# One norm extraction for a pair of second-layer weight blocks, and moved steps of attention tiles

## The chip, the cores and the metric

One Trainium2 chip, one core. The metric is the device time of one execution in microseconds (us). The engines are TensorE (matmul; PE in the profile, PEld for its weight loads), VectorE (DVE), ScalarE (ACT), GpSimd (POOL) and SyncE (SP, whose queue issues nearly all DMAs).

## The reference

```python
# attention: batch 2, 8 heads, 576 positions, head width 64, the 32 largest scores of a row kept
scores = matmul(q, k.T) / 8
kth = partition(scores, -32)[..., -32]
scores = where(scores >= kth, scores, -1e9)
attn = exp(scores - max); attn = attn / (sum(attn) + 1e-9)
x = (attn @ v)            # -> 1152 tokens x 512
# first layer pair, 512 -> 2048 -> 512
h = x @ w_in
x = (maximum(h, 0) + alpha * minimum(h, 0)) @ w_out
# second layer pair, 512 -> 1536 -> 512
out = ((x @ w_a) * (x @ w_b)) @ w_out2
```

## The kernel before

Three strands of work run side by side and are written into one program by a small planner (`step`, at the end): it keeps a clock for each strand, always takes the strand whose clock with its shift (`SHIFT_ATT`, `SHIFT_BG`) is lowest, and thereby gives out the instructions in an order. The compiler's scheduler then orders each engine's queue by that order as a priority, among what is ready by its own estimate of times; `tc.high_priority(offset=HPM)` moves the instructions inside it ahead by HPM places.

Strand `dve_track` holds the conversion of the weights and attention. The weights come as 64-bit words of 128 x 512 blocks. `to_f32` loads one block (`raw`, L190), makes the low part on ScalarE (`rlo`, L195 and L196), shifts the high part on VectorE (L197) and adds on GpSimd (L198). There are 68 blocks: 16 each of `wi` and `wo` (first layer), 12 each of `wa`, `wb` and `w2` (second). `CONV` is their order. `square` multiplies a block by its own transpose on TensorE (`gram`, L210) and takes the sum of the diagonal with one VectorE instruction (`junk`, L215), the extraction. Blocks of `wi` and `wo` share one sum for two blocks; each block of `wa` and `wb` has an extraction of its own out of a shared bank and `prep_out` adds the two; each block of `w2` has its own gram and extraction. `w2` blocks don't stay in SBUF: they are stored to DRAM (`w_st`, L222) from one of three slots (`w2s`, W2B = 3), and loaded again (L743) into the same slots when the second layer reads them. The grams share two PSUM banks (tag Y) with the layers' accumulators.

Attention goes through 72 tiles of 128 query rows. `middle` is the search on VectorE: four times the eight largest (L451, L460) and three times their replacement (L458), with a step boundary k = 0 to 7 after each; then masking (L467), the sum's reciprocal, and the normalised row on GpSimd (L474). While tile i is searched, other tiles' work is given out at fixed steps: the scores of the next tile (`front`, L440, copied by L443) at KFRONT; the transposes of the tile before (`back`, L501 to L504) and, at a pair's end, the product with v (`av`, L535) at KBACK. For the second batch ("lifted" tiles, from tile 36 on) the transpose is a DMA (L496) at KLIFT, and the product (L530) comes in the tile after that, at KAV. `v_pair` loads and splits v of the second batch for two heads, in the tiles that V_AT names, at step KV.

Strand `mlp` holds the layers, in six groups of 128 or 256 tokens: `moe1` (L615, L619 and L627, L630 for the two products) and `moe2` (hab or ha and hb, then o). Their epilogues on ScalarE, VectorE and GpSimd (`r`, `gp_n`, `gt`, `gp`) are the instructions under HPM; the end of a group, `finish` (`yb`, L690 to L706), is under HPY = 0. Strand `bg` splits converted weights in two 16-bit halves (`pair`) after the first groups have used them.

Of the kernel before, what the change touches and what calls it, by code (L numbers as in the profile page):

```python
# [11 lines left out]
BF16 = mybir.dt.bfloat16  # L12
# [5 lines left out]
ALU = mybir.AluOpType  # L18

P = 128  # L20
# [5 lines left out]
NF1 = F1 // P  # L26
NF2 = F2 // P
# [1 line left out]
NEG = -3.0e38  # L29

LIFT = 2.0 ** 14
KLIFT = 3
KAV = 3
KV = 4
V_AT = {20: 0, 26: 1, 38: 2, 40: 3}
NORM = "pool"
RLOB = 3
W2B = 3
# [8 lines left out]
JB = 1  # L47
# [15 lines left out]
M2M = 'ppd'  # L63
F0 = 1
HPY = 0
HPM = 100
SB = 2
KBACK = 2
KFRONT = 2
SHIFT_ATT = 4.0  # L70
SHIFT_BG = 4.0
T_PAIR = 4.0
T_ATT = 6.1
# [1 line left out]
F_PE = 1.1  # L75

STEPS = 9
CONV = [(n, i) for i in range(NF1) for n in ("wi", "wo")] + [(n, i) for i in range(NF2) for n in ("wa", "wb", "w2")]
PASSES = ((0, 0), (0, 1), (1, 0))
NBLK = {"wi": NF1, "wo": NF1, "wa": NF2, "wb": NF2, "w2": NF2}  # L80

NPART = {"wi": NF1 // 2, "wo": NF1 // 2, "wa": NF2 // 2, "wb": NF2 // 2, "w2": NF2}


@with_exitstack
def tile_topk_attention_moe(ctx: ExitStack, tc: tile.TileContext, qT, kT, vM, vL, wi, wo, al, wa, wb, w2, out):
    nc = tc.nc
    cp = ctx.enter_context(tc.tile_pool(name="cp", bufs=1))
    sp = ctx.enter_context(tc.tile_pool(name="sp", bufs=2))
# [4 lines left out]
    def psum(name, tag="H"):  # L94
        return pp.tile([P, 512], F32, tag=tag, name=name, bufs=2)

    def small(name, k=1):
        return cp.tile([P, k], F32, tag=name, name=name)

    ident = cp.tile([P, P], F32, tag="ident", name="ident")  # L100
# [11 lines left out]
    def pow2(ssq, scale, inv, k):  # L112
        e2 = sp.tile([P, k], I32, tag=f"e2_{k}", name="e2", bufs=2)
        nc.vector.tensor_scalar(e2[:, 0:k], ssq.bitcast(I32), 1, 0x7F800000, op0=ALU.logical_shift_right, op1=ALU.bitwise_and)
        nc.vector.tensor_scalar(scale.bitcast(I32), e2[:, 0:k], -1, 204 << 23, op0=ALU.mult, op1=ALU.add)
        nc.vector.tensor_scalar(inv.bitcast(I32), e2[:, 0:k], 50 << 23, None, op0=ALU.add)

    def totals(part, k):
        ps = psum("tot")
        nc.tensor.matmul(ps[:, 0:k], ones, part, start=True, stop=True)  # L120
        t = sp.tile([P, NF1], F32, tag="tot", name="tot_s", bufs=2)
        nc.vector.tensor_copy(t[:, 0:k], ps[:, 0:k])
        return t[:, 0:k]
# [4 lines left out]
    def row_max(dst, part):  # L128
        m = sp.tile([P, 2], F32, tag="rm", name="rm", bufs=2)
        fold(m[:, 0:1], part, ALU.max)  # L130
        ps = psum("rmt")
        nc.tensor.matmul(ps[0:1, 0:P], m[:, 0:1], ident, start=True, stop=True)
        fold(m[0:1, 1:2], ps[0:1, 0:P], ALU.max)
        ps2 = psum("rmb")
        nc.tensor.matmul(ps2[:, 0:1], ones[0:1, :], m[0:1, 1:2], start=True, stop=True)
        nc.vector.tensor_copy(dst, ps2[:, 0:1])
# [29 lines left out]
    wsb, wsc, winv, parts = {}, {}, {}, {}  # L166
    for name in ("wi", "wo", "wa", "wb"):
        wsb[name] = cp.tile([P, NBLK[name], DM], F32, tag=f"{name}_sb", name=f"{name}_sb")
    all_parts = small("parts", sum(NPART.values()))
    k0 = 0  # L170
    for name, nb in NBLK.items():
        parts[name] = all_parts[:, k0:k0 + NPART[name]]
        k0 += NPART[name]
        k = 1 if name in ("wo", "w2") else nb // 2
# [4 lines left out]

    def w2_tile():  # L180
        return sp.tile([P, DM], F32, tag="w2s", name="w2s", bufs=W2B)
    cols = {"s": small("cols", 2 * NF2)}
    srcs = {"wi": wi, "wo": wo, "wa": wa, "wb": wb, "w2": w2}
    w2_tiles = {}

# [2 lines left out]
    def to_f32(dst, name, i):  # L188
        raw = early.tile([P, DM], I64, tag="raw", name="raw", bufs=RAWB)
        nc.sync.dma_start(raw, srcs[name][i])  # L190
        lo = raw.bitcast(U32).rearrange("p (n t) -> p n t", t=2)[:, :, 0]
        hi = raw.bitcast(I32).rearrange("p (n t) -> p n t", t=2)[:, :, 1]
        d = dst.bitcast(I32)
        r = early.tile([P, DM], I32, tag="rlo", name="rlo", bufs=RLOB)
        nc.scalar.activation(r.bitcast(I16).rearrange("p (n t) -> p n t", t=2)[:, :, 0], lo, AF.Copy, scale=2.0 ** -29)  # L195
        nc.scalar.activation(r.bitcast(BF16).rearrange("p (n t) -> p n t", t=2)[:, :, 1], hi.bitcast(F32), AF.Sign)  # L196
        nc.vector.tensor_scalar(d, hi, 3, None, op0=ALU.logical_shift_left)  # L197
        nc.gpsimd.tensor_tensor(out=d, in0=d, in1=r, op=ALU.add)  # L198

    def square(name, i, src, n):
        own = name in ("wa", "wb")
        gram = psum("gram", "Y")
        w = src.bitcast(BF16).rearrange("p b (n t) -> p b n t", t=2)[:, :, :, 1]
        for f in range(n):
            d = gram[:, f * P:(f + 1) * P] if own else gram[:, 0:P]
            for c in range(4):
                x = w[:, f, c * P:(c + 1) * P]
                nc.tensor.matmul(d, x, x, start=c == 0 and (own or f == 0), stop=c == 3 and (own or f == n - 1))  # L210
        k = 2 * i + (NF2 if name == "wb" else 0)
        for f in range(2 if own else 1):
            to = cols["s"][:, k + f:k + f + 1] if own else parts[name][:, i:i + 1]
            junk = sp.tile([P, P], BF16, tag="junk", name="junk", bufs=JB)
            nc.vector.scalar_tensor_tensor(junk, gram[:, f * P:(f + 1) * P], 4.125, ident, op0=ALU.mult, op1=ALU.mult, accum_out=to)  # L215

    def block(name, i):
        if name == "w2":
            t = w2_tile()
            to_f32(t, name, i)  # L220
            square(name, i, t.unsqueeze(1), 1)
            nc.sync.dma_start(w2_st[i], t)  # L222
        else:
            to_f32(wsb[name][:, i], name, i)
            if i % 2:
                square(name, i // 2, wsb[name][:, i - 1:i + 1], 2)

    def halves(name, f):
        v = (w2_tiles[f] if name == "w2" else wsb[name][:, f]).bitcast(F16)
# [2 lines left out]
    def scales(name, common):  # L232
        nb = NPART[name]
        t = totals(parts[name], nb)
        if common:
            q = sp.tile([P, 2], F32, tag="rm", name="fold", bufs=2)
            fold(q[:, 0:1], t, ALU.add)
            pow2(q[:, 0:1], wsc[name], winv[name], 1)
        else:
            pow2(t, wsc[name], winv[name], nb)  # L240
        nc.vector.tensor_scalar(wsc[name], wsc[name], 2.0, None, op0=ALU.mult)
        return t
# [59 lines left out]
        nc.vector.tensor_mul(back_y, back_y, winv["wo"][:, 0:1])  # L302

    def prep_out():
        for j, name in enumerate(("wa", "wb")):
            s = cols["s"][:, j * NF2:(j + 1) * NF2].rearrange("p (n t) -> p n t", t=2)
            nc.vector.tensor_add(parts[name], s[:, :, 0], s[:, :, 1])
        scales("wa", False)
        scales("wb", False)
        scales("w2", True)  # L310

        q = small("pq", 4)
        ab = small("pab", NF2)
        nc.vector.tensor_mul(ab, cols["s"][:, 0:NF2], cols["s"][:, NF2:2 * NF2])
        row_max(q[:, 0:1], ab)
        pow2(q[:, 0:1], q[:, 1:2], q[:, 2:3], 1)
        nc.vector.tensor_scalar(q[:, 1:2], q[:, 1:2], 2.0 ** -30, None, op0=ALU.mult)
        nc.vector.tensor_scalar(pre["wa"], winv["wa"], q[:, 1:2], None, op0=ALU.mult)
        nc.vector.tensor_scalar(back_o, winv["w2"][:, 0:1], q[:, 2:3], 2.0 ** 30, op0=ALU.mult, op1=ALU.mult)
# [53 lines left out]
    for g, grp in enumerate(M1):  # L373
# [6 lines left out]
        for part, hp in [(p, h) for p in ((grp[:1], grp[1:]) if lead else (grp,)) for h in range(4)]:  # L380
# [6 lines left out]
            for unit in units:  # L387
                pts_of = {}
                for slot, (kind, b, t) in enumerate(unit):
                    n = P if kind == "T" else D  # L390
# [157 lines left out]
    def attention():  # L548
# [11 lines left out]
        for i, tl in enumerate(tiles):  # L560
            s = ready.pop(0)
            for k, _ in enumerate(middle(tl, s)):
                if k == 0 and i + FA < len(tiles):
                    fetch(tiles[i + FA])
                if k == 1 and i + VA < len(tiles):
                    fetch_v(tiles[i + VA])
                if k == KV and i in V_AT:
                    v_pair(V_AT[i])
                if k == KAV and due:
                    p = due.pop(0)  # L570
                    av(p)
                    yield ("done", p[0]["g"], len(p))
                if prev is not None and k == (KLIFT if prev["lift"] else KBACK):
                    back(prev)
# [4 lines left out]
                    elif prev["last"]:  # L579
                        av(pr)  # L580
                        yield ("done", prev["g"], len(pr))
                        pr = []
                if k == KFRONT and i + QA < len(tiles):
                    ready.append(front(tiles[i + QA]))
# [49 lines left out]
    def moe1(g, s1, s2):  # L634
# [9 lines left out]
        def l1(fc):  # L644
# [6 lines left out]
            contract(h, "wi", fc, xT, n, s1)  # L651
            with tc.high_priority(offset=HPM):
                if s2:
# [76 lines left out]
    def moe2(gs, s3, s4):  # L730
# [32 lines left out]
        def l3(f):  # L763
# [10 lines left out]
            for g, yT, t0 in parts:  # L774
                n = gsize[g]
                va, vb = ha[:, t0 * P:t0 * P + n], hb[:, t0 * P:t0 * P + n]
                with tc.high_priority(offset=HPM):
                    a = sized("r1", 2, n, s4)
# [60 lines left out]
    clock = {"dve": 0.0, "mlp": 0.0, "bg": 0.0}  # L839
# [16 lines left out]
    def dve_track():  # L856
        att = attention()
        cnt = [0] * len(M1)
        need = [sum(1 for t in tiles if t["g"] == g) for g in range(len(M1))]
        order = iter(CONV)  # L860

        def convert():
            name, i = next(order)
            block(name, i)
            conv_done[name, i] = clock["dve"] + T_CONV
            if (name, i) == CONV[-1]:
                open_late()
# [83 lines left out]
    live = {"dve", "mlp", "bg"}  # L951
    shift = {"dve": -SHIFT_ATT, "mlp": 0.0, "bg": SHIFT_BG}

# [8 lines left out]
            clock[k] += r  # L962
        return True

    clock["bg"] = 50.0
    while live:
        step(min(live, key=lambda k: clock[k] + shift[k]))

# [41 lines left out]
```

## Time and profile before

| what | us |
|---|---|
| median of 3 runs | 708.64 |
| lowest and highest | 707.94, 713.67 |
| the profiled execution | 712.79 |
| its span, first to last instruction | 711.0 |
| busy in the span: TensorE, VectorE | 613.9, 565.2 |
| busy in the span: ScalarE, GpSimd | 471.2, 441.9 |

The span is one execution. Times inside it are compared with each other; its own 712.79 us belongs to it and lies above the median of the runs. A busy time is a mean over stretches with different limits.

### The profile page before, as it was taken

The numbers are of one execution on the slowest core, as the hardware profiler recorded it, in microseconds if no ns is written. First come the engines' busy times: TensorE is split into PE (matmuls) and PEld (weight loads), VectorE is DVE, ScalarE is ACT, GpSimd is POOL, SyncE is SP. The second block draws the span as 40 slices with busy tenths as digits, with TensorE's granted clock in tenths as the row PEclk, the third lists the DMA queues.
The fourth block names the chain that finished last, engine by engine and source line by source line (L and its number), as shares of the span: only waits on it lengthen the run. The fifth ranks groups of instructions, "written<-read, shape, count | busy, mean of one in ns | idle before, by whom it ended". The sixth has DMA issues, their size and how long they took to land.

```text
span 711.0 us, 14959 instructions
## 1 busy us (share of the span) xinstructions
PE 613.9 (86%) x5094; PEld 458.4 (64%) x5094; DVE 565.2 (79%) x1450; ACT 471.2 (66%) x979; POOL 441.9 (62%) x648
## 2 busy tenths in 40 slices
PE   2455758899989897979976999999799999999997
PEld 1344545678766576756745777775777766677775
DVE  3998899879889989888999889999999998321021
ACT  4867988797588977789788644466555555543232
POOL 5766788888466667779888854565366555223221
PEclk9976669999989998999998999999899999999999
DMA  6986899895440031222267754523245622001243
GB/s 169 326 236 197 305 318 292 285 359 161 141 123 25 12 84 53 81 73 79 77 196 198 186 143 98 122 42 65 42 102 111 135 54 51 18 2 45 74 130 109
DMA packets 98493, 94.58 MB, mean 133 GB/s; under 512 B 50416, under 2 KB 72688, under 8 KB 98416
## 3 DMA queue, kind: packets, MB, share of 16 engines
q1 hardware_dynamic: 97104, 91.26, 45.3%
q10 hardware_dynamic: 1312, 2.36, 1.1%
q8 instruction: 40, 0.66, 0.4%
q14 instruction: 37, 0.30, 0.1%
HBM read 74.33 MB, written 8.65 MB: 117 GB/s over the span
## 4 chain that ended last, share of the span: by engine, by line
PE 54%; DVE 19%; ACT 10%; DMA 8%; issue 5%; POOL 2%; SPq 1%; ACTq 0%; POOLq 0%; DVEq 0%
PE hab L615 14%; PE h L615 7%; PE o L627 7%; PE y L627 6%; DVE wk L458 5%; DVE m L460 4%; PE ps L440 3%; PE o L535 3%; PE o L630 2%; PE hb L619 2%; DMA kr<-in_kT_dram 2%; PE ha L619 2%; DVE e L467 2%; PE o L530 2%; PE y L630 2%
## 5 line engine op out<-in xcount | busy, mean ns | idle before, releaser
L460 DVE MAX8 m<-wk 128x8 f32<-128x576 f32 x216 | 163.0, 755 | 2.2
L606 POOL TENSOR_TENSOR gp<-gt,gp 128x256 f16<-128x256 f32 (+1 forms) x112 | 67.5, 610 | 84.9 <-ACT gp L605 73.5
L458 DVE MATCH_REPLACE8 wk<-m,wk 128x576 f32<-128x576 f32 x144 | 106.9, 742 | 0.0
L615 PE MATMUL h<-xT,wi_sb 128*128 128x256 f16 (+1 forms) x960 | 97.1, 254 | 3.5 <-ACT xT L543 1.6
L615 PEld LDWEIGHTS <-wi_sb 128*128 128x128 f16 x960 | 79.3, 99 | 22.9 <-issue 9.5
L627 PEld LDWEIGHTS <-gp 128*128 128x128 f16 x588 | 54.8, 98 | 56.4 <-POOL gp L606 3.3
L627 PE MATMUL y<-wo_sb,gp 128*128 128x512 f16 x336 | 81.5, 380 | 2.8 <-POOL gp L606 1.6
L474 POOL TENSOR_SCALAR e<-e,sm 128x576 f32<-128x576 f32 x72 | 54.7, 760 | 45.0 <-DVE sm L472 40.6
L440 PE MATMUL ps<-ks,qh 128*128 128x288 f32 x160 | 48.0, 383 | 30.8 <-DVE e L467 21.7
L615 PE MATMUL hab<-xT,wa_sb 128*128 128x256 f16 (+1 forms) x648 | 69.0, 254 | 1.3 <-ACT xT L706 1.1
L451 DVE MAX8 m<-s 128x8 f32<-128x576 f32 x72 | 54.1, 752 | 18.0 <-ACT s L443 17.4
L605 ACT ACTIVATE gp<-gt 128x256 f16<-128x256 f32 (+1 forms) x112 | 42.2, 388 | 38.5 <-DVE gt L788 18.4
L615 PE MATMUL hab<-xT,wb_sb 128*128 128x256 f16 (+1 forms) x648 | 67.0, 251 | 0.0
L615 PEld LDWEIGHTS <-wa_sb 128*128 128x128 f16 x648 | 54.4, 100 | 14.7 <-issue 1.5
L627 PE MATMUL o<-w2s,gp 128*128 128x512 f16 x252 | 62.8, 379 | 1.0 <-DMA w2s<-w_pr 0.9
L788 DVE SCALAR_TENSOR_TENSOR gt<-hab,wb_inv,r 128x256 f32<-128x256 f32 (+1 forms) x36 | 15.6, 434 | 60.3 <-ACT r L782 60.2
L467 DVE SCALAR_TENSOR_TENSOR e<-s,m,ep 128x576 f32<-128x576 f32 x72 | 58.1, 808 | 3.9 <-PE t L503 1.3
L615 PEld LDWEIGHTS <-wb_sb 128*128 128x128 f16 x648 | 53.1, 99 | 5.8 <-issue 0.4
L195 ACT ACTIVATE rlo<-raw 128x512 int16<-128x512 uint32 x68 | 53.8, 792 | 4.1 <-DMA raw<-in_wi_dram 3.0
L464 ACT ACTIVATE ep<-s,nb 128x576 f32<-128x576 f32 x72 | 53.9, 749 | 3.4 <-DVE e L467 1.7
L782 ACT ACTIVATE r<-hab,pre_wa 128x256 f32<-128x256 f32 (+1 forms) x48 | 21.4, 445 | 51.0 <-PE hab L615 51.0
L440 PEld LDWEIGHTS ps<-ks,qh 128*128 128x128 f32 x160 | 28.6, 210 | 40.7 <-DVE e L467 20.3
(206 smaller groups left out, 1462.3 us busy)
## 6 DMA issues: line engine op xcount, KB each, us to landing
w2s<-w_pr SPq DMA_DIRECT2D x48, 256.0 KB, 2.7
w2s<-w_st SPq DMA_DIRECT2D x36, 256.0 KB, 2.8
raw<-in_wi_dram SPq DMA_DIRECT2D x16, 512.0 KB, 7.0
raw<-in_wo_dram SPq DMA_DIRECT2D x16, 512.0 KB, 6.8
raw<-in_wa_dram SPq DMA_DIRECT2D x12, 512.0 KB, 5.0
raw<-in_wb_dram SPq DMA_DIRECT2D x12, 512.0 KB, 5.1
raw<-in_w_dram SPq DMA_DIRECT2D x12, 512.0 KB, 5.0
kr<-in_kT_dram SPq DMA_DIRECT2D x32, 144.0 KB, 3.1
```

The lines of the kernel that those rows point to most:

```text
L195: nc.scalar.activation(r.bitcast(I16).rearrange("p (n t) -> p n t", t=2)[:, :, 0], lo, AF.Copy, scale=2.0 ** -29)
L440: nc.tensor.matmul(ps[:, f, 0:HALF], q[:, h % 2, :], ks[h][:, f * HALF:(f + 1) * HALF], start=i == 0, stop=i == len(mm) - 1)
L451: nc.vector.max(m8[:, 0:8], s)
L458: nc.vector.match_replace(out=wk, in_to_replace=m8[:, 8 * r - 8:8 * r], in_values=src, imm_value=NEG)
L460: nc.vector.max(m8[:, 8 * r:8 * r + 8], wk)
L464: nc.scalar.activation(ep, w2(s), AF.Exp, bias=nb, scale=0.125)
L467: nc.vector.scalar_tensor_tensor(w2(e), w2(s), m8[:, 31:32], ep, op0=ALU.is_ge, op1=ALU.mult, accum_out=sm[:, 0:1])
L474: nc.gpsimd.tensor_scalar(e, e, sm[:, 1:2], 1.0, op0=ALU.mult, op1=ALU.mult)
L605: nc.scalar.activation(h[:, 0:n], t[:, 0:n], AF.Copy)
L606: nc.gpsimd.tensor_sub(l[:, 0:n], t[:, 0:n], h[:, 0:n])
L615: nc.tensor.matmul(dst[:, 0:n], w[a][:, c * P:(c + 1) * P], x[:, b, c, 0:n], start=k == 0, stop=k == 11)
L627: nc.tensor.matmul(dst, act[b][:, s], w[a], start=i == 0 and k == 0, stop=i == last and k == 2)
```

## The change

Each pair of blocks of `wa`, `wb` and `w2` now shares one sum: one gram of eight matmuls into one place and one extraction, as for `wi` and `wo`; 34 extractions instead of 52. The second-layer conversions come in pairs of blocks (wa, wa, wb, wb, w2, w2), and of `w2` the first block's slot is kept until the second is there. Eight constants of the planner change.

```diff
-KLIFT = 3
-KAV = 3
-KV = 4
-V_AT = {20: 0, 26: 1, 38: 2, 40: 3}
+KLIFT = 4
+KAV = 2
+KV = 6
+V_AT = {22: 0, 28: 1, 38: 2, 40: 3}
-HPM = 100
+HPM = 400
-KBACK = 2
-KFRONT = 2
-SHIFT_ATT = 4.0
+KBACK = 4
+KFRONT = 1
+SHIFT_ATT = 3.0
-CONV = [...] + [(n, i) for i in range(NF2) for n in ("wa", "wb", "w2")]
+CONV = [...] + [(n, i) for j in range(0, NF2, 2) for n in ("wa", "wb", "w2") for i in (j, j + 1)]
-NPART = {..., "wa": NF2 // 2, "wb": NF2 // 2, "w2": NF2}
+NPART = {..., "wa": NF2 // 2, "wb": NF2 // 2, "w2": NF2 // 2}
-    def square(name, i, src, n):
-        own = name in ("wa", "wb")
+    def square(name, i, src):
         gram = psum("gram", "Y")
...
-        for f in range(2 if own else 1):
-            to = cols["s"][:, k + f:k + f + 1] if own else parts[name][:, i:i + 1]
-            junk = sp.tile([P, P], BF16, tag="junk", name="junk", bufs=JB)
-            nc.vector.scalar_tensor_tensor(junk, gram[:, f * P:(f + 1) * P], 4.125, ident, op0=ALU.mult, op1=ALU.mult, accum_out=to)
+        for f, t in enumerate(src):
+            w = t.bitcast(BF16).rearrange("p (n t) -> p n t", t=2)[:, :, 1]
+            for c in range(4):
+                x = w[:, c * P:(c + 1) * P]
+                nc.tensor.matmul(gram[:, 0:P], x, x, start=c == 0 and f == 0, stop=c == 3 and f == len(src) - 1)
+        junk = sp.tile([P, P], BF16, tag="junk", name="junk", bufs=JB)
+        nc.vector.scalar_tensor_tensor(junk, gram[:, 0:P], 4.125, ident, op0=ALU.mult, op1=ALU.mult, accum_out=parts[name][:, i:i + 1])
+    held = []
     def block(name, i):
         if name == "w2":
             t = w2_tile()
             to_f32(t, name, i)
-            square(name, i, t.unsqueeze(1), 1)
             nc.sync.dma_start(w2_st[i], t)
+            held.append(t)
         else:
             to_f32(wsb[name][:, i], name, i)
-            if i % 2:
-                square(name, i // 2, wsb[name][:, i - 1:i + 1], 2)
+            held.append(wsb[name][:, i])
+        if i % 2:
+            square(name, i // 2, held[-2:] if name == "w2" else [wsb[name][:, i - 1], wsb[name][:, i]])
     def prep_out():
-        for j, name in enumerate(("wa", "wb")):
-            s = cols["s"][:, j * NF2:(j + 1) * NF2].rearrange("p (n t) -> p n t", t=2)
-            nc.vector.tensor_add(parts[name], s[:, :, 0], s[:, :, 1])
...
-        ab = small("pab", NF2)
-        nc.vector.tensor_mul(ab, cols["s"][:, 0:NF2], cols["s"][:, NF2:2 * NF2])
+        ab = small("pab", NF2 // 2)
+        nc.vector.tensor_mul(ab, parts["wa"], parts["wb"])
-    clock["bg"] = 50.0
+    clock["bg"] = 30.0
```

## Rows read from the trace of the kernel before

**Rows 1.** Busy time by stretch: from:to, length, PE, PEld, DVE, ACT, POOL, clock, DMA.

```profile
98.00:126.60 28.60, 18.57 (x116) 13.68 (x114) 28.60 (x67) 23.24 (x49) 25.64 (x29) 0.86 0.91 294
126.60:200.00 73.40, 71.25 (x554) 56.91 (x555) 61.83 (x201) 58.69 (x127) 55.23 (x68) 0.98 0.69 228
200.00:400.00 200.00, 174.30 (x1412) 129.62 (x1410) 180.55 (x453) 167.07 (x340) 151.59 (x236) 0.94 0.34 93
400.00:602.00 202.00, 195.93 (x1650) 143.31 (x1648) 194.44 (x466) 108.54 (x225) 113.31 (x184) 0.98 0.43 93
```

**Rows 2.** Chain of waits in order of time: start, us, what.

```profile
126.62 2.07 PE h L619 x8
...
609.80 0.90 PE o L530 x27
```

**Rows 3.** Groups of VectorE instructions: count, busy us, mean ns of one, idle before.

```profile
L460 DVE MAX8 m<-wk 128x8 f32<-128x576 f32 x216 | 163.0, 755 | 2.2
...
L215 DVE SCALAR_TENSOR_TENSOR junk<-gram,ident 128x128 bf16<-128x128 f32 x52 | 14.6, 280 | 6.4 <-PE gram L210 6.2
```

**Rows 4.** VectorE in order of time: start us, us, what.

```profile
115.68 0.28 DVE L215 SCALAR_TENSOR_TENSOR junk<-gram,ident 128x128 bf16<-128x128 f32 x1
...
115.96 1.52 DVE L197 TENSOR_SCALAR w2s<-raw 128x512 int32<-128x512 int32 x1
```

**Rows 5.** GpSimd in order of time at the same place.

```profile
115.91 1.29 POOL L198 TENSOR_TENSOR wb_sb<-wb_sb,rlo 128x512 int32<-128x512 int32 x1 [0.93 <-ACT rlo L196]
```

**Rows 6.** Waits of TensorE from 99 us on: us in total, times, longest.

```profile
PE tp L705 <- ACT yb L700: 5.9, 4, 4.3
PE ps L440 <- DVE e L467: 5.1, 3, 3.2
PE h L619 <- DVE gp_n L669: 3.6, 2, 2.4
...
PE o L530 <- DMA pt<-e: 2.9, 3, 2.1
...
PE t L501 <- POOL e L474: 2.3, 2, 1.4
PE gram L210 <- DVE junk L215: 2.1, 2, 1.7
PE y L627 <- POOL gp L606: 1.6, 2, 0.8
```

**Rows 7.** Busy time in the stretches of half clock, first and last of six.

```profile
126.30:129.70 3.40, 3.08 (x16) 3.02 (x17) 2.83 (x11) 2.65 (x7) 2.44 (x3) 0.50 0.89 265
...
501.80:508.60 6.80, 5.69 (x49) 5.38 (x47) 6.33 (x16) 3.76 (x6) 1.90 (x4) 0.50 0.12 22
sum 34.00, PE 29.59 PEld 25.13 DVE 31.03 ACT 24.35 POOL 18.53; mean PE 4.93 PEld 4.19 DVE 5.17 ACT 4.06 POOL 3.09
```

**Rows 8.** Waits of VectorE from 200 to 602 us.

```profile
DVE m L451 <- ACT s L443: 10.3, 12, 2.3
```

**Rows 9.** DMA issues: count, size, median us from issue to landing.

```profile
w2s<-w_st SPq DMA_DIRECT2D x36, 256.0 KB, 2.8
...
pt<-e SPq DMA_TRANSPOSE x36, 3.2
```

**Rows 10.** Waits of SyncE's queue over the span.

```profile
SPq L496 <- ACT e L480: 61.3, 23, 6.0
```

**Rows 11.** TensorE in order of time, last second-layer conversions.

```profile
180.47 1.12 PE L630 MATMUL o<-w2s,gp_n 128*128 128x512 f32 x2 [1.18 <-DMA w2s<-w_st]
...
183.44 1.02 PE L630 MATMUL o<-w2s,gp_n 128*128 128x512 f32 x2
...
191.63 0.40 PE L210 MATMUL gram<-w2s 128*128 128x128 bf16 x4
```

**Rows 12.** Tile `w2s` from 98 to 205 us: ns min/median/max, first and last start.

```profile
L630 PE MATMUL o<-w2s,gp_n x24: 590/592/697, 164.2 to 201.1; 128*128 128x512 f32 x24
...
L197 DVE TENSOR_SCALAR w2s<-raw x12: 409/856/1524, 103.1 to 175.4; 128x512 int32<-128x512 int32 x12
```

More of the change, by code (lines that the diff above doesn't have):

```diff
@@ L77 @@
 STEPS = 9
-CONV = [(n, i) for i in range(NF1) for n in ("wi", "wo")] + [(n, i) for i in range(NF2) for n in ("wa", "wb", "w2")]
+CONV = [(n, i) for i in range(NF1) for n in ("wi", "wo")] + [(n, i) for j in range(0, NF2, 2) for n in ("wa", "wb", "w2") for i in (j, j + 1)]
 PASSES = ((0, 0), (0, 1), (1, 0))
 NBLK = {"wi": NF1, "wo": NF1, "wa": NF2, "wb": NF2, "w2": NF2}
-NPART = {"wi": NF1 // 2, "wo": NF1 // 2, "wa": NF2 // 2, "wb": NF2 // 2, "w2": NF2}
+NPART = {"wi": NF1 // 2, "wo": NF1 // 2, "wa": NF2 // 2, "wb": NF2 // 2, "w2": NF2 // 2}
 @with_exitstack
@@ L181, in w2_tile @@
         return sp.tile([P, DM], F32, tag="w2s", name="w2s", bufs=W2B)
-    cols = {"s": small("cols", 2 * NF2)}
     srcs = {"wi": wi, "wo": wo, "wa": wa, "wb": wb, "w2": w2}
@@ L198, in to_f32 @@
         nc.gpsimd.tensor_tensor(out=d, in0=d, in1=r, op=ALU.add)
-    def square(name, i, src, n):
-        own = name in ("wa", "wb")
+    def square(name, i, src):
         gram = psum("gram", "Y")
-        w = src.bitcast(BF16).rearrange("p b (n t) -> p b n t", t=2)[:, :, :, 1]
-        for f in range(n):
-            d = gram[:, f * P:(f + 1) * P] if own else gram[:, 0:P]
+        for f, t in enumerate(src):
+            w = t.bitcast(BF16).rearrange("p (n t) -> p n t", t=2)[:, :, 1]
             for c in range(4):
-                x = w[:, f, c * P:(c + 1) * P]
-                nc.tensor.matmul(d, x, x, start=c == 0 and (own or f == 0), stop=c == 3 and (own or f == n - 1))
-        k = 2 * i + (NF2 if name == "wb" else 0)
-        for f in range(2 if own else 1):
-            to = cols["s"][:, k + f:k + f + 1] if own else parts[name][:, i:i + 1]
-            junk = sp.tile([P, P], BF16, tag="junk", name="junk", bufs=JB)
-            nc.vector.scalar_tensor_tensor(junk, gram[:, f * P:(f + 1) * P], 4.125, ident, op0=ALU.mult, op1=ALU.mult, accum_out=to)
+                x = w[:, c * P:(c + 1) * P]
[3 more added lines that the diff above has]
+    held = []
     def block(name, i):
```

## The prediction

> **What bounds the kernel now.** I read the stretch table first [rows 1]; the reader is to see which column comes nearest to the length of its row. Before 98 us the first layer's weights are converted and attention starts; the change touches little there. From 98 to 126.6 us VectorE has no idle time at all (28.60 of 28.60) and TensorE waits for it. From 126.6 to 200 us TensorE has 71.25 of 73.4 us. From 200 to 400 us both are loose: TensorE idles 25.7 us, VectorE 19.5. From 400 to 602 us both are full (idle 6.1 and 7.6 us). The chain of waits says the same: it passes from VectorE to TensorE at 126.62, and near the end it is TensorE [rows 2]. The last attention product, at 609.80, is at once followed by the layers' work, so both engines come to that point together. Hence a gain must be one on both: VectorE work that goes is worth nothing where TensorE has no idle time to give.
>
> The waits of TensorE tell what there is to win after 99 us [rows 6]: many small ones of 1 to 6 us in sum. Some are paid twice: after such idle time the granted clock is 0.50 for a while, six times from 126 us on, 34.0 us in all, from 126.30 for 3.4 us to 501.80 for 6.8 us [rows 7]. At 1.2 in place of 2.4 GHz a busy TensorE does half the work, so these cost up to 17 us, 3.4 us for each long one.
>
> **Extractions.** 18 of 52 go. One takes 0.28 us [rows 3], and its accumulator read lies inside the time to the next starts (115.68 to 115.96 with a small operation between, [rows 4]): 18 x 0.28 = 5.0 us of VectorE, in the stretch in which the second layer's weights are converted. The two additions that go with them are single small operations there; nothing. What of the 5.0 us lies on the path? Behind 126.6 us the chain is not on VectorE, and what is saved becomes idle time. Ahead of that stand six extractions of the second layer (one is that at 115.68, [rows 4]), of which three go: 0.84 us. The matmuls of a gram also wait for an extraction, 2.1 us in two waits [rows 6], since grams share two banks with the layer's accumulator, and one gram in place of two halves the turns for `w2`. I take half of that, 1.0 us. The bound of the gain is 0.84 + 2.1 = 2.9 us; the other end is a loss, the rival of the slots below. Taken: -1.8.
>
> [Rows 4, 5] show a shift of 1.52 us at 115.96, while GpSimd's addition ran from 115.91 for 1.29 us; the fastest shift of this kind took 0.41 us [rows 12]. The Trainium skill (SBUF — State Buffer, "Who interferes with whom") says that such a VectorE operation and a GpSimd operation hold one port pair exclusively, whoever starts first, and the trace agrees with 1.52 against 0.41 us. By that rule an extraction ahead of a blocked shift frees nothing, since the shift ends with the addition; three of the six have a shift behind them, and the 0.84 would be 0.42.
>
> **Order of conversion.** An even block of `wb` comes third of six instead of second, one of `w2` fifth instead of third. The twelve `w2` shifts run from 103.1 to 175.4 [rows 12], eleven rounds of three conversions, 2.2 us each. The cover is the conversions' lead: the second layer multiplies its first `w2` block at 164.2 [rows 12], when some ten of twelve are made. Nothing; 2 x 2.2 = 4.4 us at one place if that lead were gone.
>
> **Transposes and products of attention (KBACK 2 to 4, KFRONT 2 to 1).** A step is one search or replacement on VectorE; a search takes 0.755 us [rows 3]. The transposes, their copies and the product at a pair's end come two steps, 1.5 us, later. TensorE stops waiting for GpSimd's normalised row: 2.3 us after 99 us [rows 6]. Against it, a group's first matmul gets its activations up to 1.5 us later. Net -0.8, bounds -2.3 and +3.0 (two group starts). In the first 98 us the conversions cover it; if that cover is gone, +1.5. The scores come one step earlier. VectorE waits 12 times, 10.3 us, for them from 200 to 602 us [rows 8]; at most 12 x 0.75 = 9.0 us go. They are worth something only where TensorE has room, from 200 to 400 us, and TensorE may now stand longer at a score that the masking of the row before still blocks (5.1 us in three waits, [rows 6]). Bounds -9.0 and +2.3 (three waits, 0.75 each); taken -2.0, nearer to the end of the three waits.
>
> **Second batch (KLIFT 3 to 4, KAV 3 to 2).** The DMA transpose is issued one step later, the product one step earlier in the tile after: 6 steps lie between them instead of 8, 6 x 0.75 = 4.5 us against 3.2 us from issue to landing [rows 9]. The cover is 1.3 us; without it 16 products could each wait up to 1.5 us, though a cover of 2.8 us now leaves only three waits, 2.9 us [rows 6]. In exchange SyncE stands less at a transpose whose input isn't ready: 61.3 us in 23 waits [rows 10], with the loads of `k`, `q` and `w2` behind it in its queue. I put it at 0, bounds -2 (two of the three waits gone) and +4.5 (three more of 1.5).
>
> **V pairs (KV, V_AT) and `clock["bg"]`.** Three DMAs on SyncE's queue, two copies on ScalarE, a subtraction and a memset on GpSimd for each of four pairs move two steps, for the first two pairs also two tiles. Their first reader is the product of tile 36; fourteen tiles of four searches and three replacements (over 5 us each by [rows 3]) cover it, and the loads behind them in the queue are issued four tiles ahead. Nothing; if the cover were gone, one landing, some 3 us. The background track gives out nothing before the last conversion is planned, so its earlier clock costs nothing.
>
> **Priority (HPM 100 to 400) and SHIFT_ATT.** The layers' epilogues go ahead of work that was given out up to 400 instructions before. What can go is what TensorE waits for them, above all 3.6 us for `gp_n` and 1.6 for GpSimd's `gp`: 5.2 us [rows 6]. The 3.6 lie where VectorE is full, so the order there decides, but a whole removal is no more likely than none. What is not lifted is the end of a group (`yb`, 5.9 us, [rows 6]), which epilogues may now pass. SHIFT_ATT puts attention 1 us later against the layers: fewer waits of TensorE for attention, more of VectorE for scores; no sign. Together -2.2, bounds -5.2 and +4.
>
> **Clock.** The waits taken above are a small part of what stands ahead of the half-rate stretches; that a long one vanishes whole is unlikely. An estimate of -0.5 us, a seventh of one; bounds 0 and -6.8 (two vanish).
>
> **The sum.** -1.8 - 0.8 - 2.0 - 2.2 - 0.5 = -7.3 us. The profiled execution took 712.79 us (span 711.0 and 1.8 around it) and would take 705.5. The median of the runs, 708.64, lies 4.15 us under that execution; 708.64 - 7.3 = **701.3**. One per cent, 7.1 us, is about what a measurement of this kernel can tell from no change.
>
> **Rivals.** *The freed time is waited away.* VectorE comes earlier to shifts that GpSimd blocks and to scores that ScalarE hasn't copied; TensorE, at 97% from 126.6 to 200 us, has no room. For it: the chain leaves VectorE at 126.62 [rows 2]. Against it: the 25.7 us of idle TensorE from 200 to 400. It gives 706 to 711.
>
> *The epilogues decide.* All 5.2 us of waits for them go, and two long half-rate stretches with them (6.8): 708.6 - 12.0 = 696.6, between 693 and 700. For it: the `gp_n` waits stand right ahead of the half-rate stretch at 126.30. Against it: the largest wait is for `yb`, which isn't lifted.
>
> *The slots of `w2` (slower).* Three slots of `w2s` serve conversions and the layer's loads. A pair now holds two until its one gram is multiplied. Before, the last shift was at 175.4 [rows 12] and its gram at 191.63 [rows 11], 16.2 us later. If a pair is held so long, the loads have one slot: 2.8 us to landing [rows 9] and 1.1 of the matmul [rows 11], 3.9 us a block against 3.0 (180.47 to 183.44, [rows 11]). 16.2 us then give 4.2 blocks instead of 5.4, 1.2 x 3.0 = 3.6 us late, and a long half-rate stretch follows the waits (3.4 us): 708.6 + 7.0 = 715.6, and more if the stretch before pays it too; 714 to 720, centre 717. It decides as soon as the pair's gram comes later than its stores land and TensorE has no other work. Against it: TensorE idled only 1.18 us for such a load [rows 11], and fewer extractions shorten the grams' turns.
>
> *It doesn't do what it says.* The 34 extractions are written out in the program; that can't fail. The steps can, if other things set the order in the queues: that is the first rival.
>
> **How the numbers follow.** Forecast 701.3, its own range 697.5 to 705, chance 0.40, 0.22 of it under 701.55 (1% faster). First rival 0.25, epilogues 0.22, slots 0.13. Faster by over 1%: 0.22 + 0.22 = 0.44. Slower: 0.13 (the slots, nearly all over 715.7). Same: 0.43. The range leaves out the slots and the last twentieth of the epilogue case: 693 to 713. The bounds of single costs, +4.5 and +4 in place of 0 and -2.2, end at 712 and lie in it.
>
> **What would show it.** Right: 34 extractions; VectorE full from 98 on, with the chain's change to TensorE 1 to 2 us earlier; TensorE idle for under 21 us between 200 and 400; fewer waits at `t`, `gp_n` and `gp`; VectorE's waits for scores under 6 us; the last attention product near 602. The slots: SyncE and TensorE waiting for `w2s` between 165 and 190 us. Wrong: a group's end (`yb`) that waits longer, or attention so late against the layers that TensorE idles ahead of the last product.

## The result and the profile after

The kernel after takes 0.9914 of the time before [0.9892, 0.9935], from interleaved runs. The quotient of the medians, 705.55 and 710.5 us, is 0.9930 and lies inside the interval. On the 708.64 us of the forecast 0.9914 is 702.5, or -6.1 us, and the interval is -4.6 to -7.7; the forecast was -7.3. The profiled execution has a span of 702.0 us against 711.0, so some 3 us of the 9.0 between these two belong to the two executions. Of these 9.0 us TensorE's busy time gives 4.0 (613.9 to 609.9) and its idle time 5.0 (97.1 to 92.1). Lines of the changed file lie about six lower: L451 is now L445, L619 is L613.

The stretch table of the kernel after (from:to, length, PE, PEld, DVE, ACT, POOL, clock, DMA), beside [rows 1]:

```profile
98.00:126.60 28.60, 22.32 (x142) 17.04 (x142) 28.35 (x68) 25.08 (x54) 25.47 (x30) 0.80 0.89 280
126.60:200.00 73.40, 68.88 (x523) 53.11 (x521) 60.82 (x163) 56.57 (x122) 55.66 (x67) 0.98 0.69 231
200.00:400.00 200.00, 177.99 (x1509) 133.57 (x1509) 186.19 (x474) 172.33 (x351) 155.44 (x246) 0.97 0.36 97
400.00:602.00 202.00, 195.82 (x1639) 139.34 (x1637) 186.70 (x448) 107.53 (x222) 113.36 (x181) 1.00 0.42 93
```

The row to look at is the third: VectorE is idle for 13.8 us instead of 19.5, TensorE for 22.0 instead of 25.7, and the clock is 0.97 instead of 0.94. From 126.6 to 200 us, where most of the extractions went, TensorE is busy for less than before (68.88 against 71.25), from 98 to 126.6 for more (22.32 against 18.57, at a lower clock). From 400 us on VectorE has more idle time than before (15.3 against 7.6), so its work is ahead by then. The chain of waits of the kernel after, beside [rows 2]:

```profile
126.45 1.21 DVE wa_sb L196
...
127.72 3.63 DMA raw<-in_wa_dram
...
132.08 0.26 DVE gp_n L663
...
132.39 0.71 PE h L613 x4
...
600.78 0.90 PE o L524 x27
```

The passage to TensorE comes at 132.39 instead of 126.62; the last product of attention comes 9.0 us earlier, the whole difference of the two executions. The extractions among VectorE's groups (count, busy, mean ns, idle before), beside [rows 3], and the shifts of tile `w2s` (ns min/median/max), beside [rows 12]:

```profile
L209 DVE SCALAR_TENSOR_TENSOR junk<-gram,ident 128x128 bf16<-128x128 f32 x34 | 9.5, 279 | 7.3 <-PE gram L207 7.3
```

```profile
L196 DVE TENSOR_SCALAR w2s<-raw x12: 409/424/952, 107.8 to 178.2; 128x512 int32<-128x512 int32 x12
```

There are 34 extractions at the same price. The last shift comes 2.8 us later than before, so the conversions did not end earlier. TensorE's waits from 99 us on, beside [rows 6], VectorE's from 200 to 602 us, beside [rows 8], and SyncE's, beside [rows 10] (us in total, times, longest):

```profile
PE ps L434 <- DVE e L461: 7.8, 9, 1.8
PE tp L699 <- ACT yb L694: 6.4, 5, 3.5
PE h L613 <- DVE gp_n L663: 4.7, 4, 2.1
PE o L524 <- DMA pt<-e: 2.8, 2, 1.9
...
PE h L609 <- DVE gp_n L663: 1.8, 2, 1.5
...
PE t L495 <- POOL e L468: 1.6, 2, 1.2
...
PE y L621 <- POOL gp L600: 1.5, 2, 0.9
...
PE gram L207 <- DVE junk L209: 0.5, 1, 0.5
```

```profile
DVE gt L650 <- ACT r L649: 7.9, 4, 4.0
DVE m L445 <- ACT s L437: 6.9, 10, 2.2
```

```profile
SPq L490 <- ACT e L474: 62.8, 21, 5.1
```

TensorE's named waits did not shrink as a set: the grams' went (2.1 to 0.5), `ps` grew (5.1 to 7.8), `gp_n` grew (at L619, now L613, 3.6 to 4.7; at L615, now L609, 0.9 to 1.8). The stretches of half clock after 126 us, beside [rows 7], are now three instead of six:

```profile
133.60:137.00 3.40, 3.40 (x18) 2.88 (x15) 2.24 (x5) 3.40 (x8) 1.87 (x2) 0.50 0.85 259
365.70:369.10 3.40, 3.30 (x34) 3.03 (x34) 3.40 (x11) 2.89 (x6) 3.40 (x5) 0.50 0.75 206
375.90:382.70 6.80, 5.35 (x44) 5.24 (x45) 6.51 (x16) 6.24 (x10) 3.66 (x4) 0.50 0.70 177
```

Where in the span the gain arises is read from the start of each tile's search (the search's first VectorE instruction, tiles counted from 0) in the two traces:

| tile | before, us | after, us | difference |
|---|---|---|---|
| 16 | 178.2 | 183.1 | +4.9 |
| 28 | 269.7 | 268.0 | -1.7 |
| 32 | 298.9 | 296.5 | -2.4 |
| 36 | 334.6 | 326.4 | -8.2 |
| 40 | 365.7 | 353.8 | -11.9 |
| 48 | 428.4 | 418.3 | -10.1 |
| 71 | 592.8 | 581.8 | -11.0 |

The layers agree (their 3468 matmuls are counted from 0 here and below): the 700th starts at 266.8 before and 267.0 after, the 800th at 300.1 and 295.2, the 1300th at 411.3 and 401.4. Until about 270 us attention only makes up for its later start; the gain arises behind that, 90 us after the last conversion, and all of it is there by 400. In that part VectorE's waits are the ones that shrank. From 290 to 420 us, before and then after:

```profile
DVE m L451 <- ACT s L443: 6.7, 7, 2.1
DVE xT L544 <- ACT xT L543: 3.7, 4, 1.8
DVE gt L788 <- ACT r L782: 3.4, 2, 2.2
```

```profile
DVE m L445 <- ACT s L437: 3.2, 6, 1.1
DVE gt L650 <- ACT r L649: 2.2, 1, 2.2
DVE xT L538 <- ACT xT L537: 1.9, 1, 1.9
```

### The profile page after: what moved, and what is told of

It is laid out like the page before. It is cut to its first block, busy times and chain, and to the rows that moved or that the text cites. A ratio compares the mean times of both kernels' runs of the same rounds, so it can differ in the third digit from the quotient of the medians.

```text
span 702.0 us, 14917 instructions
## 1 busy us (share of the span) xinstructions
PE 609.9 (87%) x5094; PEld 453.0 (65%) x5094; DVE 561.2 (80%) x1412; ACT 472.1 (67%) x979; POOL 441.7 (63%) x648
## 4 chain that ended last, share of the span: by engine, by line
PE 46%; DVE 20%; ACT 8%; DMA 8%; issue 5%; POOL 4%; SPq 0%; DVEq 0%; ACTq 0%; POOLq 0%
PE hab L609 9%; PE h L609 8%; PE y L621 6%; DVE wk L452 6%; DVE m L454 5%; PE o L621 5%; PE ps L434 3%; DVE e L461 3%; PE hb L613 2%; PE ha L613 2%; DMA pt<-e 2%; PE o L624 2%; DVE m L445 2%; PE y L624 2%; PE o L529 1%
## 5 line engine op out<-in xcount | busy, mean ns | idle before, releaser
L609 PE MATMUL h<-xT,wi_sb 128*128 128x256 f16 (+1 forms) x960 | 97.1, 251 | 4.4 <-DVE gp_n L663 1.8
L609 PEld LDWEIGHTS <-wi_sb 128*128 128x128 f16 x960 | 78.2, 98 | 23.9 <-issue 9.6
L609 PE MATMUL hab<-xT,wa_sb 128*128 128x256 f16 (+1 forms) x648 | 68.8, 252 | 0.3 <-DVE gt L782 0.3
L609 PE MATMUL hab<-xT,wb_sb 128*128 128x256 f16 (+1 forms) x648 | 66.2, 251 | 0.0
L445 DVE MAX8 m<-s 128x8 f32<-128x576 f32 x72 | 54.0, 751 | 13.6 <-ACT s L437 13.2
L782 DVE SCALAR_TENSOR_TENSOR gt<-hab,wb_inv,r 128x256 f32<-128x256 f32 (+1 forms) x36 | 15.7, 435 | 58.8 <-ACT r L776 58.7
L609 PEld LDWEIGHTS <-wa_sb 128*128 128x128 f16 x648 | 53.6, 100 | 13.4 <-issue 0.4
L609 PEld LDWEIGHTS <-wb_sb 128*128 128x128 f16 x648 | 52.8, 99 | 5.8 <-issue 0.4
L776 ACT ACTIVATE r<-hab,pre_wa 128x256 f32<-128x256 f32 (+1 forms) x48 | 21.4, 445 | 48.5 <-PE hab L609 48.5
```

The source lines that it names most:

```text
L445: nc.vector.max(m8[:, 0:8], s)
L609: nc.tensor.matmul(dst[:, 0:n], w[a][:, c * P:(c + 1) * P], x[:, b, c, 0:n], start=k == 0, stop=k == 11)
```

## The experiments

All ratios are to the kernel before, with 95% intervals; the kernel after is at 0.9914. "Idle" is VectorE's from 290 to 420 us (130 less its busy time), the measure that the first eight runs suggested.

| kernel | ratio | interval | span, us | idle, us |
|---|---|---|---|---|
| before | 1 | | 711.0 | 15.8 |
| after | 0.9914 | 0.9892 to 0.9935 | 702.0 | 10.7 |
| struct_only | 0.9979 | 0.9955 to 1.0003 | 706.2 | 12.8 |
| const_only | 1.0047 | 1.0019 to 1.0075 | 712.1 | 16.8 |
| after_kback2 | 1.0075 | 1.0048 to 1.0102 | 716.5 | 21.7 |
| after_shift4 | 1.0129 | 1.0093 to 1.0165 | 721.2 | 22.5 |
| after_hpm100 | 0.9896 | 0.9869 to 0.9924 | 702.2 | 11.4 |
| after_klift3 | 0.9922 | 0.9900 to 0.9944 | 703.6 | 12.5 |
| after_idle | 0.9915 | 0.9883 to 0.9946 | 703.2 | 14.4 |
| after_twice | 1.0133 | 1.0094 to 1.0173 | 725.2 | 22.1 |
| after_core | 0.9985 | 0.9956 to 1.0014 | 706.9 | 15.9 |
| after_kf2 | 0.9977 | 0.9950 to 1.0004 | 710.0 | 17.9 |
| after_shift35 | 1.0014 | 0.9988 to 1.0039 | 709.3 | 15.6 |
| after_conv | 1.0070 | 1.0044 to 1.0097 | 714.9 | 20.7 |

**The two halves of the change.** struct_only is the kernel after with all constants back, as below; const_only is the kernel before with the same lines the other way round.

```diff
-KLIFT = 4
-KAV = 2
-KV = 6
-V_AT = {22: 0, 28: 1, 38: 2, 40: 3}
+KLIFT = 3
+KAV = 3
+KV = 4
+V_AT = {20: 0, 26: 1, 38: 2, 40: 3}
...
-HPM = 400
+HPM = 100
...
-KBACK = 4
-KFRONT = 1
-SHIFT_ATT = 3.0
+KBACK = 2
+KFRONT = 2
+SHIFT_ATT = 4.0
...
-    clock["bg"] = 30.0
+    clock["bg"] = 50.0
```

struct_only: 

> The pair sums and the new order of conversion, with all eight constants as before. The prediction's sum gives this part -1.8 us: ratio to before 0.997 to 0.998, with 34 extractions and VectorE's busy time 4 to 5 us lower. First rival (the freed time is waited away): 0.999 to 1.001, with the same busy time gone. Second rival (the pair sums carry the whole gain): 0.990 to 0.993. Slots rival: 1.005 or more, with TensorE waiting for w2s between 165 and 190 us.

const_only: 

> The eight constants as after, with 52 extractions and the conversion order of before. The prediction's sum gives the constants -5.5 us: 0.992, with TensorE idle under 21 us between 200 and 400 us. If the pair sums carry the gain: 0.998 to 1.000. If neither part has a price of its own and the order in the queues as a whole decides, the two parts' ratios don't multiply to the whole change's 0.991.

The fewer extractions (with their order of conversion) alone give -1.5 us, with 0 inside the interval; the constants alone cost 3.3 us. Together 0.9979 x 1.0047 = 1.0026 was to come, and 0.9914 came. The gain belongs to neither half; 1.1% of it is there only when both are.

**The extractions' own cost.** The 18 second-layer extractions are made twice; the second one writes the same sum over the first.

```diff
+        for _ in range(2 if name in ("wa", "wb", "w2") else 1):
-        nc.vector.scalar_tensor_tensor(junk, gram[:, 0:P], ...)
+            nc.vector.scalar_tensor_tensor(junk, gram[:, 0:P], ...)
```

> The changed kernel with each of the 18 second-layer extractions done twice (same operands and result), so with the 52 VectorE extractions of before, but with pair sums and the order of conversion of after. The prediction's 0.28 us each adds 5.0 us to VectorE's busy time; on the path it said 0.84 us or so: ratio 0.991 to 0.995. If freed VectorE time there carries the gain: 0.998 or more, with the loss already seen in the layers' progress at 200 us. If order decides: off to either side, with the layers' progress at 200 us within 3 us of the changed kernel's.

From 98 to 200 us VectorE is busy for 93.28 us instead of 89.17, 4.1 us more, near the 5.0 that were put back:

```profile
98.00:200.00 102.00, 91.20 (x662) 70.15 (x661) 89.17 (x230) 81.65 (x174) 81.12 (x96) 0.93 0.75 245
```

```profile
98.00:200.00 102.00, 91.42 (x683) 71.28 (x682) 93.28 (x273) 82.65 (x178) 81.78 (x97) 0.94 0.77 254
```

(The kernel after comes first.) Yet the last shift starts at 178.2 in both, and the layers' 600th matmul at 247.3 instead of 246.2, the 700th at 268.7 instead of 267.0. By the 800th it is 5.1 us (300.3 against 295.2), and in the span 23. So less than 2 us are lost until 270 us, and some 21 us behind that, where no extraction stands. The added instructions also change the order: with all extractions left out of the count, 643 of the other 1344 VectorE instructions stand at another place in the queue than in the kernel after. That the order is the cause is argued from this and not shown by itself. Read as the price of extractions, this run would have misled.

**The steps KBACK and KFRONT.**

```diff
-KBACK = 4
-KFRONT = 1
+KBACK = 2
+KFRONT = 2
```

> The changed kernel with KBACK and KFRONT back at 2. By the prediction's sum the two steps are worth -2.8 us: the ratio to before rises from 0.991 to 0.995, TensorE waits again for GpSimd's normalised row after 99 us (over 2 us) and VectorE for scores over 8 us between 200 and 602 us. If the steps do nothing: 0.991. If the order decides: a ratio off by more than 0.5% to either side, with the change at the group ends or at the scale chain around 270 us and not at the transposes.

It gives back 1.6%, 11 us, and more than the whole gain. Against the kernel after, tile 40 starts 1.4 us later and tile 44 16.2 us later: one place. VectorE there, in order of time (start, us, what, idle before and releaser), and the chain at the same place:

```profile
390.19 0.76 DVE L454 MAX8 m<-wk 128x8 f32<-128x576 f32 x1
395.28 0.48 DVE L782 SCALAR_TENSOR_TENSOR gt<-hab,wb_inv,r 128x256 f32<-128x256 f32 x1 [4.32 <-ACT r L776]
...
399.80 0.48 DVE L782 SCALAR_TENSOR_TENSOR gt<-hab,wb_inv,r 128x256 f32<-128x256 f32 x1 [2.88 <-ACT r L776]
403.74 0.48 DVE L782 SCALAR_TENSOR_TENSOR gt<-hab,wb_inv,r 128x256 f32<-128x256 f32 x1 [3.45 <-ACT r L776]
404.21 0.76 DVE L445 MAX8 m<-s 128x8 f32<-128x576 f32 x1
```

```profile
388.95 1.11 POOL w2s L252
...
391.08 3.06 DMA w2s<-w_st
...
394.90 2.96 DMA w2s<-w_st
...
398.70 3.01 DMA w2s<-w_st
...
402.48 2.78 DMA w2s<-w_pr
```

A search ends at 390.95, and the next instructions of VectorE's queue are the layers' epilogues (L782), which ScalarE's `r` (L776) releases; the chain runs through the splitting of `w2` (L252 with its loads, and L250 on ScalarE). VectorE stands 4.32, 2.88 and 3.45 us at them, and the next search, of tile 44, starts at 404.21 behind them. But they are not what holds it. Its scores are copied by ScalarE only at 403.54 and it starts 0.03 us after that copy ends; in the kernel after the copy comes at 387.21. TensorE and then ScalarE of after_kback2, in order of time:

```profile
395.48 0.29 PE L434 MATMUL ps<-ks,ql 128*128 128x288 f32 x1
395.81 1.47 PE L609 MATMUL hab<-xT,wa_sb 128*128 128x256 f16 x12
...
399.74 1.47 PE L609 MATMUL hab<-xT,wb_sb 128*128 128x256 f16 x12
400.97 0.38 PE L434 MATMUL ps<-ks,ql 128*128 128x288 f32 x1
```

```profile
401.73 0.72 ACT L250 ACTIVATE wsc<-w2s,w_sc 128x512 f32<-128x512 f32 x1 [2.03 <-DMA w2s<-w_st]
...
403.54 0.64 ACT L437 ACTIVATE s<-ps 128x576 f32<-128x576 f32 x1
```

The last of the four matmuls of these scores starts 5.5 us after the third, behind 48 matmuls of the layers, and the copy then stands in ScalarE's queue behind a split of `w2` (L250), which had waited for its load, and an `r`. In the kernel after the four run together, from 386.30 to 387.07. So at this place the time goes into the order on TensorE and ScalarE, and the search could not have started before 404.18 wherever the epilogues stood. The waits of that kernel from 290 to 420 us:

```profile
DVE gt L782 <- ACT r L776: 11.1, 4, 4.3
DVE xT L538 <- ACT xT L537: 4.5, 5, 1.6
DVE m L445 <- ACT s L437: 4.1, 6, 1.5
```

By this table scores (`m`) are hardly waited for more than after (4.1 against 3.2), but it names the instruction at which the engine stood, and a late score hides behind an epilogue that is late as well. KFRONT alone set back:

```diff
-KFRONT = 1
+KFRONT = 2
```

> The changed kernel with KFRONT alone back at 2. VectorE's queue is that of the changed kernel up to row 555 of 1087. If the earlier scores are what the two steps brought: ratio 1.000 or more, like 1.008 of both steps back, with VectorE waiting for scores or layers between 290 and 420 us. If KBACK brought it: 0.991 within 0.003. Span by the waiting theory: 702 + 1.6 x (VectorE's idle time from 290 to 420 us - 10.7), within 4 us.

It costs 0.6%, 4.5 us, with 17.9 us of idle VectorE, between the two values expected. VectorE's queue first differs from that of the kernel after at 395 us, and most of the loss follows there: tile 44 is 2.2 us late, tile 48 8.9.

**SHIFT_ATT.** after_shift4 sets it back, after_shift35 half of the way.

```diff
-SHIFT_ATT = 3.0
+SHIFT_ATT = 4.0      # after_shift35: 3.5
```

after_shift4: 

> The changed kernel with SHIFT_ATT back at 4. The prediction gives it no sign: 0.991 within 0.002. If the planner's order as a whole decides: off by 0.5% or more, although no instruction is added or removed.

after_shift35: 

> The changed kernel with SHIFT_ATT = 3.5, half way to the 4 that gave 1.013. If a later attention is a cost or gain by itself: 1.002, between the two. If the order it leads to is what counts: nothing binds it to lie between 0.991 and 1.013. Span by the waiting theory: 702 + 1.6 x (VectorE's idle time from 290 to 420 us - 10.7), within 4 us.

Set back whole it costs 2.1%, 15 us; half, 1.0%. This is the largest single effect of a constant, of the one to which the prediction gave no sign. Half the step costs half, 1.0014 where "a cost or gain by itself" was to give 1.002, so this run agrees with a price of this constant beside the other new ones; the reading by order forbade nothing here and is not tested by it. With 3.0 attention stands 1 us later against the layers in the order than with 4.0, and yet VectorE waits less.

**HPM, KLIFT and KAV, V pairs.** Three single undoings:

```diff
after_hpm100
-HPM = 400
+HPM = 100
after_klift3
-KLIFT = 4
-KAV = 2
+KLIFT = 3
+KAV = 3
after_idle
-KV = 6
-V_AT = {22: 0, 28: 1, 38: 2, 40: 3}
+KV = 4
+V_AT = {20: 0, 26: 1, 38: 2, 40: 3}
...
-    clock["bg"] = 30.0
+    clock["bg"] = 50.0
```

after_hpm100: 

> The changed kernel with HPM back at 100. Its queues differ from the changed kernel's in 29 of 1087 VectorE rows, all of them past row 999, so past 550 us. The prediction's sum gave HPM and SHIFT_ATT together -2.2 us, which would bring the ratio to before from 0.991 to 0.994. If a price follows what the queues do: 0.991 within 0.002, since TensorE waits for nothing there.

after_klift3: 

> The changed kernel with KLIFT and KAV back at 3: the second batch's transposes one step earlier, its products two steps later. The prediction gives it 0, bounds +2 and -4.5: 0.991, from 0.985 to 0.994. If the order of GpSimd and ScalarE between 350 and 400 us decides (attention of tiles 36 to 47 beside the splitting of w2): a ratio off by 0.005 or more with all of it between those times.

after_idle: 

> The changed kernel with KV, V_AT and the background clock back: only the loads of v for the second batch move, which the prediction costs at nothing: 0.991 within 0.002. Rival: the order decides, and as the queues differ in 640 VectorE rows from about 170 us on, the ratio is off by 0.005 or more though no work and no wait was added at the moved step.

None costs anything by its interval. Places in VectorE's queue, counted in the traces by source line and tile name (1412 instructions; the expectations count otherwise), tell why for two of them: after_hpm100 has 9 at another place than the kernel after, all past 578 us, and after_klift3 17. after_idle has 343 and costs nothing either, so a moved queue is no loss by itself; after_kf2 with fewer, 254, costs 0.6%. But after_core undoes the three together:

```diff
-KLIFT = 4
-KAV = 2
-KV = 6
-V_AT = {22: 0, 28: 1, 38: 2, 40: 3}
+KLIFT = 3
+KAV = 3
+KV = 4
+V_AT = {20: 0, 26: 1, 38: 2, 40: 3}
...
-HPM = 400
+HPM = 100
...
-    clock["bg"] = 30.0
+    clock["bg"] = 50.0
```

> The pair sums and new order of conversion with KBACK, KFRONT and SHIFT_ATT alone; the other constants as before. If these three carry the constants' part: ratio to before 0.991 within 0.003. If the order as a whole decides: off by more. In either case the theory formed since, that the time follows how long VectorE waits between 290 and 420 us (10.7 us of it in the changed kernel's 702.0 us span, 15.8 in 711.0), gives the profiled span as 702 + 1.6 x (that idle time - 10.7), within 4 us.

0.9985: three zeros make 0.7%, 5 us. A zero of a single undoing is no property of that constant.

**The order of conversion.** Back to one block of each weight in turn, with the sums of pairs kept.

```diff
-... + [(n, i) for j in range(0, NF2, 2) for n in ("wa", "wb", "w2") for i in (j, j + 1)]
+... + [(n, i) for i in range(NF2) for n in ("wa", "wb", "w2")]
```

> The changed kernel with the conversions back in the order wa, wb, w2 of one block after the other, the pair sums kept. The prediction put the order at 0: 0.991 within 0.003. If the slots of w2 mattered: better than 0.991 or, with the first block of a pair kept over four other conversions, worse by 3 us or more already at 200 us. Span by the waiting theory: 702 + 1.6 x (VectorE's idle time from 290 to 420 us - 10.7), within 4 us.

It costs 1.6%, 11 us, and tells most about where the strands meet. With this order the layers are far ahead of the kernel after at their 800th matmul (285.5 against 295.2), and behind it at the 900th (329.0 against 325.3). In between they wait for attention: tile 36 starts at 328.6, against 326.4. 9.7 us won by the layers before 290 us were worth nothing.

All fourteen traces show the layers standing at the same place, between their matmuls 833 and 834, where the first layer of a group begins on what attention has made (in after_conv TensorE does attention's work meanwhile). The gap is 7.6 us in the kernel after and 8.9 before, but 20.5 in after_conv and 22.4 in after_shift4 (13.0 in const_only, 11.5 in after_twice, 6.8 to 9.3 in the others). after_conv comes to it 10.5 us ahead of the kernel after and leaves it 2.4 behind (311.7 against 309.3), after_shift4 4.3 ahead and 10.5 behind: the lead is waited away there, and more. In after_kback2 the gap is 8.6 us, so its loss is another one.

**What the runs have in common.** The rows from 290 to 420 us of before, after, after_shift4 and after_twice, in this order (columns as in the stretch table), each from its own kernel's trace:

```profile
290.00:420.00 130.00, 113.24 (x1016) 84.59 (x1016) 114.24 (x277) 102.06 (x208) 106.11 (x173) 0.96 0.49 133
```

```profile
290.00:420.00 130.00, 115.71 (x1033) 86.47 (x1032) 119.31 (x291) 103.34 (x204) 108.16 (x173) 0.96 0.52 136
```

```profile
290.00:420.00 130.00, 104.67 (x885) 77.20 (x884) 107.54 (x261) 95.85 (x191) 98.24 (x161) 0.86 0.47 120
```

```profile
290.00:420.00 130.00, 110.73 (x986) 83.11 (x986) 107.93 (x264) 101.24 (x202) 105.34 (x169) 0.95 0.44 114
```

After the first eight runs I fitted the span by VectorE's idle time in this stretch: 702 + 1.6 x (idle - 10.7). It meets nine of those ten kernels within 4.7 us and after_twice within 5.0. The last four runs were forecast by it, before they ran, as within 4 us: measured less formula -3.4 (after_core), -3.5 (after_kf2), -0.5 (after_shift35) and -3.1 (after_conv). All four hold, all on the same side, so the slope is somewhat steep. It is a weak test: each forecast used the idle time of the very trace, and a constant 710 us would have met three of the four within 4 us and the fourth within 5. TensorE's idle time in the same stretch does worse: 13.8 us in after_kf2 (span 710.0) and 18.3 in after_idle (703.2). The granted clock there does not order them either: before and after both have 0.96, and after_twice, the longest, 0.95. Five kernels lose clock as well (0.92 to 0.86: after_kf2, after_kback2, after_conv, const_only, after_shift4), so the clock adds to a loss, but it doesn't decide which kernel has one.

The fit says where time is lost and not which engine paces. VectorE's busy time over the whole span is nearly the same in all fourteen (558 to 568 us), so a longer span must have more idle VectorE somewhere. A slope of 1.6 leaves a part of it outside the stretch, and there the idle time differs too, from 125 to 136 us. TensorE's idle time over the whole span, 91.8 to 109.1 us, tells the span as well, within 4.2 us of a straight line.

## Why the prediction was right, and where it was right for other reasons

**Sign, size and range held**: -6.1 us against -7.3, 702.5 within 697.5 to 705, and the last attention product at 600.78 against "near 602". The number is in part luck. The sum gave the extractions -1.8 us and the constants -5.5; by themselves the extractions gave -1.5 (interval -3.2 to +0.2) and the constants +3.3, the wrong way. What makes -6.1 of them is 7.9 us that come only with both together, for which the sum has no term. The terms do not add in the other direction either: the single undoings of KBACK with KFRONT (11), SHIFT_ATT (15) and the order of conversion (11) cost 37 us, and only 6.1 were gained.

**What bounds.** "A gain must be one on both" engines, and the room is from 200 to 400 us: right. VectorE lost 5.6 us of idle time there and TensorE 3.7. "TensorE idle for under 21 us" missed by 1.0.

**Extractions, -1.8.** By itself about the right size (-1.5 us, struct_only, not told from 0). The place was wrong: the chain's change to TensorE was to come 1 to 2 us earlier and came 5.8 us later, and putting the work back costs under 2 us until 270 us (after_twice). The grams' waits fell by 1.6 us, 2.1 to 0.5, where 1.0 was priced. The Trainium skill (SBUF — State Buffer, "Who interferes with whom") bears on the shifts beside them. By it a shift and a GpSimd operation can block each other through the ports that the two share; the traces agree in that each shift of over 0.5 us, 39 of 68 before and 41 of 68 after, runs beside a GpSimd instruction (of the quicker ones 18 of 29 and 16 of 27 do too). For `w2s` the median fell from 0.856 [rows 12] to 0.424 us, but over all 68 shifts it did not (0.6 us in both), so the shifts as a whole got no faster.

**Order of conversion, 0.** Failed: "the cover is the conversions' lead" looked at the conversion stretch alone, where indeed nothing is lost; undone by itself in the kernel after (after_conv), the order costs 11 us, all after 290 us, where the layers wait for attention.

**KBACK and KFRONT, -0.8 and -2.0.** Sign right, size short: undone in the kernel after, they cost 11 us, 4.5 of it by KFRONT alone, against -11.3 as the sum of their lower bounds. The named mechanisms are the smaller part: waits for scores fell by 3.4 us (10.3 to 6.9, the forecast was under 6), those at `t` by 0.7. In after_kback2 12 of the 16.2 us by which tile 44 is late arise at that tile, whose scores are late on TensorE and ScalarE. That is the wait the term named, but as an order behind the layers' matmuls and a split, not as a step of 0.75 us.

**KLIFT and KAV, V pairs and the background's clock, 0 each.** Right one at a time (0.9922 and 0.9915), wrong for a group of them (after_core, 5 us).

**HPM and SHIFT_ATT, -2.2.** The term had its two halves the wrong way round. HPM does nothing (0.9896 without it, 9 moved instructions), and the waits for `gp_n` it was to take away grew. SHIFT_ATT, "no sign", is the largest single lever in the kernel after. The reason given, fewer waits of TensorE against more of VectorE, failed: undone, both engines wait more, VectorE 22.5 us and TensorE 25.3 us (130 - 104.67) from 290 to 420, where the kernel after has 10.7 and 14.3, and the layers stand 22.4 us for attention.

**Clock, -0.5.** Mis-sized: half-rate stretches after 126 us fell from 34.0 to 13.6 us, and TensorE's busy time by 4.0 us. The bound of -6.8 would have held that, but what of the span the clock gave back no run separates.

**The rivals.** "The freed time is waited away" holds for the conversion stretch, but not for the program. The epilogues and the slots did not come: waits at a group's end stayed (5.9 to 6.4 us), and TensorE waited 0.6 us for loads of `w2s` from `w_st`, 1.2 before.

**What stands, and what is open.** Shown: the gain arises between 270 and 400 us; the time of fourteen kernels follows VectorE's idle time from 290 to 420 us; layers that are ahead win nothing there. Shown for one place each: what is late in after_kback2 (the scores of tile 44) and where the layers of after_conv and after_shift4 lose their lead (the gap). Argued only: that such waits are the cause of the gain itself, since no run changed them with the order of the queues kept; in after_twice an added instruction reordered the queues as well. Open: why one order has 10.7 us of such waits and its neighbour 22; the prediction did not foresee it from the steps that the constants name. No single undoing beats the kernel after beyond its interval; after_hpm100, 0.9896, overlaps it.

## What to carry to other kernels

Where a planner orders the queues, prices of single edits add up only if the order stays: first count how many instructions change their place (9 and 17 of 1412 were no change in time, hundreds were anything from 0 to 2%), and treat the rest as a set that is measured whole. Find the places where two strands meet, and read there which strand stands and for how long: one gap in the layers, 7.6 us or over 20, showed where two kernels lost their lead. A table of waits names the instruction at which an engine stood. Before calling that the cause, look up when the inputs of the next instructions were there: the epilogue at which VectorE stood for 4.32 us was not what kept the search behind it.

## What the runs showed of the hardware that was not expected

A half-rate stretch need not show as a delay. The kernel after runs at half clock (0.50) from 92.6 to 109.7 us, the kernel before at 0.61 in the mean of the same stretch, and yet the layers' 100th matmul comes at 127.3 us against 130.7 before:

```profile
92.60:109.70 17.10, 12.56 (x58) 9.71 (x58) 16.56 (x38) 15.36 (x32) 14.27 (x16) 0.50 0.90 298
```

VectorE has 16.56 us of the 17.10, TensorE 12.56 even at half rate, so TensorE had room. That the stretch costs nothing is not shown: the kernel before was at half clock for most of it too, other things changed with it, and what it would give at full rate was not tried.
